# Another order of TensorE's and ScalarE's work in the last head of a cached-attention decode kernel

## The chip, the cores and the metric

The kernel runs on one core of a Trainium2 chip. The metric is the device time of one launch in microseconds (us). A core has five engines that run side by side, each through its own instructions in order: TensorE (PE: matmuls, with PEld for its weight loads), VectorE (DVE), ScalarE (ACT), GpSimd (POOL) and SyncE (SP, which here issues the loads from device memory). They meet only at semaphores.

## The reference, cut to what matters

One token is decoded. A block of attention over a cache of 32768 positions is followed by a small dense block:

```python
H, Sk, Dh, D, Dff = 32, 32768, 192, 640, 1536
q = (layernorm(x) @ wq).reshape(1, 1, H, Dh).transpose(0, 2, 1, 3)
p = softmax(einsum("bhqd,bhkd->bhqk", q, k_cache) * Dh ** -0.5)
o = einsum("bhqk,bhkd->bhqd", p, v_cache)
h = x + o.transpose(0, 2, 1, 3).reshape(1, 1, H * Dh) @ wo
out = h + relu(layernorm(h) @ w1) @ w2
```

All inputs are bf16. The two caches hold 32 heads x 32768 rows x 192 elements each, 805 MB together, and every element is used once. The page counts 824.97 MB read.

## The kernel before, in words

**One head.** The 32768 keys of a head lie on 128 partitions with 256 keys each. The work is cut into chunks: a chunk c is `jc` keys of every partition. Its scores are made in two ways. For the first `jc - jp` keys VectorE multiplies the keys by the query (L695) and sums each product (L698), into the tile `sc`. For the other `jp` keys TensorE transposes the keys (L373, into one of four PSUM tiles `tp`, four 128x128 blocks to a tile), ScalarE copies the transposed blocks to SBUF (L598, `kT`, two buffers by the chunk's parity), and TensorE multiplies them by the query (L354, into the one tile `sp`). ScalarE takes the exponentials of both parts (L604 from `sp` into `pB`, L613 from `sc` into `pA`) and sums them into `dsums` as it goes. TensorE then adds the value rows weighted by the exponentials (L354, `o_ps<-va,pB` and `o_ps<-va,pA`). The exponentials need no maximum, so a head has no second pass. The sum of the exponentials comes from a matmul with a matrix of ones (`den_mm`), its reciprocal from VectorE (L703, L704), which also scales the result (L710, `o_pair`); TensorE turns the pair of rows into a column (`o_turn`), VectorE copies that (L716, L720, `oT`), and TensorE multiplies it by `wo` (`project`) into the running sum `attT`.

**Order.** Heads 0 to 30 are a loop with a fixed order of eight chunks. The last head (`LAST`, 31) is written out in `pe_end` for TensorE, in the last part of `act_head` for ScalarE and in `dve_head` for VectorE. In what follows the steps of its ten chunks have short names, which the changed code uses too: T3 is `transposes` of chunk 3, C3 the copies of those blocks, S3 the `scores_pe` of chunk 3, E3 the exponential of TensorE's scores (`exp_pe`), D3 the exponential of VectorE's scores (`exp_dve`), P3 the value sums of chunk 3 (`values`), O the turn of the head before. P8 comes in two parts, P8a (the part of TensorE's scores) and P8b (the part of VectorE's); `den_mm` of the last head stands between them. Per chunk, `jp` is 16, 16, 20, 16, 20, 16, 12, 12, 8, 8 and VectorE's part is 16, 16, 12, 16, 12, 16, 8, 8, 8, 0 keys of a partition. So T and C have 12, 12, 15, 12, 15, 12, 9, 9, 6, 6 blocks, S has 24, 24, 30, 24, 30, 24, 18, 18, 12, 12 matmuls, and P has 16 matmuls in chunks 0 to 5, 10 in chunks 6 and 7, 8 in chunk 8 and 4 in chunk 9.

**What waits for what.** T waits for the keys and for the copy of the tile that used its PSUM bank four tiles earlier. C waits for its T. S waits for its last copy and for E of the chunk before, as there is one `sp`. E waits for S. D waits for VectorE. P waits for E and D of its chunk and for its values; P0 also waits until the head before has been scaled out of `o_ps` (L710). VectorE does its scores chunk after chunk; after chunk 0 it does L703, L704 and L710 of the head before, after chunk 2 it does L716 and L720, for which it needs O. VectorE waits for P0 before chunk 8 too.

**Loads.** All are issued by SyncE in one order (L235). For the last head: keys of chunks 0 and 1, values of chunks 0 and 1, keys of 2 and 3, keys of 4 and 5, values of 2 and 3, keys of 6 and 7, of 8, of 9, values of 4, of 5. Then come the values of chunks 6, 7, 8 and 9, which go over those of chunks 0 and 1 and so wait for P1 (L297); then the last piece of `wo`; then `w1` and four cuts of `w2` (6, 3, 2 and 1 of its 12 row blocks), which go over the keys of chunks 0 to 3 and wait for P3 (L303). GpSimd passes on the landing of the loads up to the values of chunk 3; for later ones TensorE and VectorE wait themselves.

**The end.** After P8b: L710, O, L720, `project`, the residual sum (L769), a layernorm (statistics by TensorE, square root by ScalarE at L626), `h1` (60 matmuls with `w1`), its relu (L668), `y` (60 matmuls with `w2`, waiting for each cut of it), the sum (L785), a transpose (L587), a copy (L671), the store (L673).

TensorE's order before, in these names: T0 T1 S0 P0 S1 T2 O P1 S2 T3 T4 S3 T5 S4 S5 P2 P3 T6 T7 S6 T8 S7 T9 S8 P4 S9 P5 P6 P7 P9 P8a den P8b. ScalarE's: C0 E0 D0 C1 E1 D1 C2 C3 E2 D2 C4 E3 C5 E4 D3 C6 E5 D4 C7 E6 C8 E7 D5 C9 E8 E9 D6 D7 D8.

Of the kernel before, what the change touches and what calls it, by code (L numbers as in the profile page):

```python
# [80 lines left out]
def kernel(  # L81
# [13 lines left out]
    P = nc.NUM_PARTITIONS  # L95

    Bsz, Sq, D = A_x.shape
# [18 lines left out]
    LAST = H - 1  # L116
# [12 lines left out]
    NCM = len(ends)  # L129
# [226 lines left out]
    def transposes(g, h, c):  # L356
        ld, off, jc, jp = chunks(h)[c][:4]
        src = k_tile(h, ld)
        if h == LAST and ld >= NL - 1:
            if c == 6 or ld >= NL:  # L360
                g.wait("k", h, ld)
        elif leads(h, c, 0):
            g.wait("at", "k", h, ld)
        t0 = sum(len(tiles(q[3])) for q in chunks(h)[:c])
        for k, (b0, nb) in enumerate(tiles(jp)):
            t = t0 + k
            dst = tp[t % TP]
            if t >= TP or h > 0:
                g.wait("cp", *tile_before(h, t))
            calls = []  # L370
            for b in range(nb):
                o = (off + jc - jp) * Dh + (b0 + b) * 2 * P
                calls.append(lambda b=b, o=o: pe.transpose(out=dst[:, b, :], in_=src[:, o:o + 2 * P].bitcast(f32),  # L373
                                                           identity=ident_f[:]))
            pe_group(g, calls, ("T", h, c, k), "pe_act")
# [11 lines left out]
    def scores_pe(g, h, c):  # L387
        ld, off, jc, jp = chunks(h)[c][:4]
        g.wait("cp", h, c, len(tiles(jp)) - 1)
        if c == 0:  # L390
            g.wait("qm", h)
        if c > 0:
            g.wait("ep", h, c - 1)
        elif h > 0:
            g.wait("ep", h - 1, NC - 1)
        src = kT[c % 2]
        calls = []
        for i in range(jp // 4):
            for b in range(3):
                for e in range(2):  # L400
                    calls.append(mmul(sp[:, 4 * i + b:4 * i + b + 2], src[:, 3 * i + b, e:2 * P:2],
                                      qm[:, 4 * b + 2 * e:4 * b + 2 * e + 2],
                                      start=(i == 0 and b == 0 and e == 0),
                                      stop=(i == jp // 4 - 1 and b == 2 and e == 1), skip_group_check=True))
        pe_group(g, calls, ("S", h, c), "pe_act")

    def values(g, h, c, part=None):


        jc, jp, ld, off = chunks(h)[c][2:]  # L410
        jd = jc - jp
        if h == LAST and ld >= NL - 1:
            g.wait("vc", h, c)
        elif h == LAST and ld == 2:
            g.wait("vh", c - 4)
        elif leads(h, c, 4):
            g.wait("at", "v", h, ld)
        g.wait("ep", h, c)
        if jd > 0 and part != 0:
            g.wait("ed", h, c)  # L420
        if c == 0 and h > 0:
            g.wait("os", h - 1)
        src = v_tile(h, ld)
        a, b = pA[c % NB], pB[c % NB]
        calls = []
        order = (list(range(jd, jc, 2)) if part != 1 else []) + (list(range(0, jd, 2)) if part != 0 else [])
        for i, j in enumerate(order):
            w = a[:, j:j + 2] if j < jd else b[:, j - jd:j - jd + 2]
            calls.append(mmul(o_ps[0:2, 0:2 * Dh], w, src[:, (off + j) * Dh:(off + j + 2) * Dh],
                              start=(c == 0 and i == 0),  # L430
                              stop=((c == NC - 1 if h < LAST else (c, part) == (NC, 1)) and i == len(order) - 1),
                              skip_group_check=True))
        pe_group(g, calls, ("PV", h, c) if part != 0 else ("PV0", h, c), "pe")
# [11 lines left out]
    def o_turn(g, h):  # L445
        g.wait("os", h)

        rows = [o_pair[:, i, :, :].rearrange("q a d -> q (a d)") for i in range(2)]
        pe_group(g, [mmul(mm[:, b:b + 1], rows[i][:, b:2 * Dh:3], ident_b[0:2, i:i + 1],
                          start=(i == 0), stop=(i == 1)) for b in range(3) for i in range(2)], ("oT", h), "pe_dve")  # L450
# [68 lines left out]
    def pe_start(g):  # L519
# [10 lines left out]
        g.wait("qe")  # L530
        q_spread(g, 0)

    def pe_end(g):
        h = LAST
        den_mm(g, h - 1)
        transposes(g, h, 0)
        transposes(g, h, 1)
        scores_pe(g, h, 0)
        values(g, h, 0)
        scores_pe(g, h, 1)  # L540
        transposes(g, h, 2)
        o_turn(g, h - 1)
        values(g, h, 1)
        scores_pe(g, h, 2)
        transposes(g, h, 3)
        transposes(g, h, 4)
        scores_pe(g, h, 3)
        transposes(g, h, 5)
        scores_pe(g, h, 4)
        scores_pe(g, h, 5)  # L550
        values(g, h, 2)
        values(g, h, 3)
        transposes(g, h, 6)
        transposes(g, h, 7)
        scores_pe(g, h, 6)
        transposes(g, h, 8)
        scores_pe(g, h, 7)
        transposes(g, h, 9)
        scores_pe(g, h, 8)
        values(g, h, 4)  # L560
        scores_pe(g, h, 9)
        for c in (5, 6, 7):
            values(g, h, c)
        values(g, h, 9)
        values(g, h, 8, 0)
        den_mm(g, h)
        values(g, h, 8, 1)
        o_turn(g, h)
        project(g, h + 1)
        st = ln_t["ln2"]["st"]  # L570
        g.wait("h_col")
        pe_group(g, [mmul(mm[:, 0:1], mean_mat[:], st[:, 0:1], start=True, stop=True)], ("mean", "ln2"), "pe_dve")
        g.wait("st", "ln2")
        pe_group(g, [mmul(sp[:, 0:2], mean_mat[:], st[:], start=True, stop=True)], ("mean2",), "pe_dve")
        g.wait("xn", "ln2")
        g.wait("w1")
        hn = ln_t["ln2"]["xn"]
        pe_group(g, [mmul(o_ps[:, f:f + 1], w1_s[:, c, f * P:(f + 1) * P], hn[:, c:c + 1],
                          start=(c == 0), stop=(c == DT - 1)) for f in range(FT) for c in range(DT)], ("h1",), "pe_act")
        g.wait("h1T")  # L580
        for i, (f0, f1) in enumerate(zip(W2_CUTS[:-1], W2_CUTS[1:])):
            g.wait("w2", i)
            pe_group(g, [mmul(attT[:, n:n + 1], w2_s[:, f, n * P:(n + 1) * P], h1T[:, f:f + 1],
                              start=(f == 0 and n == 0), stop=(f == FT - 1 and n == DT - 1), skip_group_check=True)
                         for f in range(f0, f1) for n in range(DT)], ("y", i), "pe_dve")
        g.wait("y_col")
        pe_group(g, [lambda: pe.transpose(out=mm[0:DT, 0:P], in_=y_col[:], identity=ident_f[:])], ("yT",), "pe_act")  # L587
# [4 lines left out]
    def copies(g, h, c):  # L592
        ld, off, jc, jp = chunks(h)[c][:4]
        t0 = sum(len(tiles(q[3])) for q in chunks(h)[:c])
        for k, (b0, nb) in enumerate(tiles(jp)):
            g.wait("T", h, c, k)
            src = tp[(t0 + k) % TP]
            g.do(lambda: act.copy(out=kT[c % 2][:, b0:b0 + nb, :], in_=src[:, 0:nb, :].bitcast(bf16)),  # L598
                 "act_pe", ("cp", h, c, k))

    def exp_pe(g, h, c):
        jp = chunks(h)[c][3]
        g.wait("S", h, c)
        g.do(lambda: act.activation(out=pB[c % NB][:, 0:jp], in_=sp[:, 0:jp], func=F.Exp, scale=SCALE,  # L604
                                    accum_out=dsums[:, 2 * c + 1:2 * c + 2]), "act_pe", ("ep", h, c))
# [29 lines left out]
    def act_head(g, h):  # L635
        q_wide(g, h)
        if h < LAST:
            for c in range(NC):
                if c == 4:
                    exp_pe(g, h, 3)  # L640
                    exp_dve(g, h, 3)
                copies(g, h, c)
                if c > 0 and c != 4:
                    exp_pe(g, h, c - 1)
                    exp_dve(g, h, c - 1)
            exp_pe(g, h, NC - 1)
            exp_dve(g, h, NC - 1)
            return

        behind = ((0,), (1,), (), (2,), (), (3,), (4,), (), (5,), ())  # L650
        for c in range(NCM):
            copies(g, h, c)
            if c < 2:
                exp_pe(g, h, c)
            elif c > 2:
                exp_pe(g, h, c - 1)
            for d in behind[c]:
                exp_dve(g, h, d)
        exp_pe(g, h, NCM - 1)
        for c in range(6, NCM):  # L660
            exp_dve(g, h, c)

    def act_end(g):
        act_head(g, LAST)
# [143 lines left out]
    for e in parts:  # L808
        far = {s: 0 for s in TAKEN[e]}
        ends_at[e] = []  # L810
        for h in range(LAST):
            for label in logs[e][h]:
                s, n = at[label]
# [90 lines left out]
```

The softmax here doesn't subtract the row's maximum and nothing guards it: scores larger than these inputs give would overflow.

## Time and profile before

| what | value |
|---|---|
| time, median of 6 runs | 1920.65 us (1919.46 to 1921.07) |
| time of the profiled execution | 1919.77 us |
| its span, first to last instruction | 1917.9 us |
| read from memory | 824.97 MB, 430 GB/s over the span |
| busy, share of the span | PE 83%, DVE 81%, ACT 49% |
| queue of the loads, share of 16 DMA engines | 99.6% |
| mean granted clock of TensorE | 0.898 |

The page gives shares over the whole span; the change touches only its last 65 us, so the views that matter are those cut to a stretch of time: the timeline of one engine (start, length, engine, line, operation, count; in brackets the idle time before it and what ended it), the chain of waits in order of time, the busy time and granted clock by stretches, and the issues of loads with the time from issue to landing. All times there are us from the start of the span.

### The profile page before, as it was taken

The numbers are of one execution on the slowest core, as the hardware profiler recorded it, in microseconds if no ns is written. First come the engines' busy times: TensorE is split into PE (matmuls) and PEld (weight loads), VectorE is DVE, ScalarE is ACT, GpSimd is POOL, SyncE is SP. The second block draws the span as 40 slices with busy tenths as digits, with TensorE's granted clock in tenths as the row PEclk, the third lists the DMA queues.
The fourth block names the chain that finished last, engine by engine and source line by source line (L and its number), as shares of the span: only waits on it lengthen the run. The fifth ranks groups of instructions, "written<-read, shape, count | busy, mean of one in ns | idle before, by whom it ended". The sixth has DMA issues, their size and how long they took to land.

```text
span 1917.9 us, 35954 instructions
## 1 busy us (share of the span) xinstructions
PE 1587.7 (83%) x15899; PEld 1003.2 (52%) x15899; DVE 1561.4 (81%) x731; ACT 936.6 (49%) x2000; POOL 1.0 (0%) x6
## 2 busy tenths in 40 slices
PE   7878888888888888788887887888888888878888
PEld 7555455555554555555554545545555555455455
DVE  2787887987878878789788888888798787887886
ACT  2454454553544544545545445445455354454454
POOL 0000000000000000000000000000000000000000
PEclk9889899898898898988888988989989889899898
DMA  9999999999999999999999999999999999999998
GB/s 408 435 438 427 436 431 433 437 429 439 431 435 437 431 437 431 434 437 432 436 432 433 438 431 436 433 433 437 431 437 429 436 435 433 436 434 433 435 428 330
DMA packets 25185, 825.28 MB, mean 430 GB/s; under 512 B 2635, under 2 KB 4172, under 8 KB 7628
## 3 DMA queue, kind: packets, MB, share of 16 engines
q1 hardware_dynamic: 25152, 824.98, 99.6%
q8 instruction: 15, 0.25, 0.0%
q14 instruction: 6, 0.05, 0.0%
q10 hardware_dynamic: 12, 0.00, 0.0%
HBM read 824.97 MB, written 0.00 MB: 430 GB/s over the span
## 4 chain that ended last, share of the span: by engine, by line
DMA 57%; DVE 37%; PE 3%; issue 1%; ACT 1%; DVEq 0%; SPq 0%; POOLq 0%
DMA kt<-in_A_k_cache_dram 51%; DVE pr L695 18%; DVE sc L698 18%; DMA va<-in_A_v_cache_dram 6%; PE o_ps L354 3%; ACT kT L598 1%; PE sp L354 0%; DVEq L65 0%; SPq L235 0%; PE attT L354 0%; PE mm L354 0%; DVE o_pair L710 0%; PE tp L373 0%; ACT pB L604 0%; POOLq L317 0%
## 5 line engine op out<-in xcount | busy, mean ns | idle before, releaser
L695 DVE TENSOR_TENSOR pr<-kt,qb 128x2304 f32<-128x2304 bf16 (+2 forms) x257 | 756.7, 2944 | 315.3 <-POOLq L317 293.9
L598 ACT COPY kT<-tp 128x1024 bf16<-128x1024 bf16 (+1 forms) x898 | 814.4, 1020 | 291.7 <-PE tp L373 291.7
L698 DVE TENSOR_REDUCE sc<-pr 128x12 f32<-128x2304 f32 (+2 forms) x257 | 756.1, 2942 | 8.9
L354 PE MATMUL o_ps<-va,pB 128*2 128x384 bf16 x2304 | 504.5, 373 | 178.8 <-POOLq L336 147.2
L373 PE MATMUL tp<-ident_f,kt 128*128 128x128 f32 x3456 | 520.7, 289 | 121.9 <-ACT kT L598 75.9
L373 PEld LDWEIGHTS tp<-ident_f,kt 128*128 128x128 f32 x3456 | 380.9, 144 | 222.4 <-ACT kT L598 169.2
L354 PEld LDWEIGHTS o_ps<-va,pB 128*2 128x2 bf16 x2304 | 199.5, 92 | 404.4 <-POOLq L336 152.6
L354 PE MATMUL o_ps<-va,pA 128*2 128x384 bf16 x1792 | 373.1, 353 | 0.0
L613 ACT ACTIVATE pA<-sc 128x12 bf16<-128x12 f32 (+2 forms) x257 | 58.9, 229 | 525.7 <-DVEq L65 525.7
L354 PEld LDWEIGHTS o_ps<-va,pA 128*2 128x2 bf16 x1792 | 162.9, 91 | 174.8 <-issue 57.1
L354 PEld LDWEIGHTS sp<-qm,kT 128*128 128x128 bf16 x6912 | 197.5, 97 | 79.3 <-ACT pB L604 30.2
L354 PE MATMUL sp<-qm,kT 128*128 128x2 bf16 x6912 | 213.2, 164 | 18.4 <-ACT pB L604 14.5
L604 ACT ACTIVATE pB<-sp 128x20 bf16<-128x20 f32 (+2 forms) x258 | 62.1, 241 | 115.0 <-PE sp L354 115.0
L604 ACT ACTIVATION_READ_ACCUMULATOR pB<-sp 128x1 f32 x258 | 64.5, 250 | 0.0
L613 ACT ACTIVATION_READ_ACCUMULATOR pA<-sc 128x1 f32 x257 | 52.8, 205 | 0.0
L354 PE MATMUL o_ps<-xn_ln,kt 128*96 128x1 bf16 (+1 forms) x316 | 22.3, 208 | 2.9 <-DMA kt<-in_A_wq_dram 2.8
L354 PEld LDWEIGHTS o_ps<-xn_ln,kt 128*96 128x96 bf16 (+1 forms) x316 | 22.2, 175 | 3.0 <-issue 2.9
L710 DVE TENSOR_SCALAR o_pair<-o_ps,rec 2x384 bf16<-2x384 f32 x32 | 19.4, 605 | 1.4 <-PE o_ps L354 0.4
L354 PEld LDWEIGHTS attT<-oT,wo_s 128*128 128x128 bf16 x465 | 13.6, 96 | 10.3 <-issue 9.9
L354 PE MATMUL attT<-oT,wo_s 128*128 128x1 bf16 x465 | 16.3, 164 | 0.3 <-DVE oT L720 0.3
L354 PEld LDWEIGHTS mm<-dsums,ones_mat 128*128 128x128 f32 x64 | 9.5, 188 | 10.6 <-issue 10.6
L703 DVE TENSOR_REDUCE rec<-mm 128x1 f32<-128x20 f32 x32 | 5.7, 179 | 10.4 <-PE mm L354 5.9
(65 smaller groups left out, 134.5 us busy)
## 6 DMA issues: line engine op xcount, KB each, us to landing
kt<-in_A_k_cache_dram SPq DMA_DIRECT2D x62, 6144.0 KB, 33.4
va<-in_A_v_cache_dram SPq DMA_DIRECT2D x62, 6144.0 KB, 20.9
kt<-in_A_k_cache_dram SPq DMA_DIRECT2D x3, 3072.0 KB, 24.6
wo_s<-in_A_wo_dram SPq DMA_DIRECT2D x16, 480.0 KB, 15.0
kt<-in_A_wq_dram SPq DMA_DIRECT2D x4, 1536.0 KB, 11.1
va<-in_A_v_cache_dram SPq DMA_DIRECT2D x2, 3072.0 KB, 27.6
va<-in_A_v_cache_dram SPq DMA_DIRECT2D x2, 1536.0 KB, 36.1
kt<-in_A_k_cache_dram SPq DMA_DIRECT2D x1, 1920.0 KB, 30.4
```

Source lines behind the costliest of these rows:

```text
L354: return lambda: pe.matmul(o, lhsT=w, rhs=r, **kw)
L373: calls.append(lambda b=b, o=o: pe.transpose(out=dst[:, b, :], in_=src[:, o:o + 2 * P].bitcast(f32), identity=ident_f[:]))
L598: g.do(lambda: act.copy(out=kT[c % 2][:, b0:b0 + nb, :], in_=src[:, 0:nb, :].bitcast(bf16)), "act_pe", ("cp", h, c, k))
L604: g.do(lambda: act.activation(out=pB[c % NB][:, 0:jp], in_=sp[:, 0:jp], func=F.Exp, scale=SCALE, accum_out=dsums[:, 2 * c + 1:2 * c + 2]), ...
L613: g.do(lambda: act.activation(out=pA[c % NB][:, 0:jd], in_=sc[c % NC][:, 0:jd], func=F.Exp, scale=SCALE, accum_out=dsums[:, 2 * c:2 * c + ...
L695: g.chain(lambda: dve.tensor_tensor(out=pr[:, 0:j1 - j0, :], in0=src[:, (off + j0) * Dh:(off + j1) * Dh].rearrange("p (j d) -> p j d", d=D ...
L698: g.chain(lambda: dve.reduce_sum(out=sc[c % NC][:, j0:j1], in_=pr[:, 0:j1 - j0, :], axis=X), "dve")
L703: g.chain(lambda: dve.reduce_sum(out=rec[:, 0:1], in_=mm[:, 0:2 * NCM], axis=X), "dve")
L710: g.do(lambda: dve.tensor_scalar_mul(out=o_pair[:, :, 1, :], in0=o_ps[0:2, 0:2 * Dh].rearrange("q (i d) -> q i d", i=2), scalar1=rec[0:2, ...
```

## The change

The hand-written order of the last head is replaced, on TensorE and on ScalarE, by two strings that a small helper walks through. No instruction is added or taken away, and no operand, load or wait of an instruction is edited; VectorE's, GpSimd's and SyncE's programs are untouched. The waits themselves follow their steps.

```diff
+    LAST_PE = "T0 T1 S0 T2 S1 T3 S2 P0 O S3 T4 T5 S4 P1 S5 P2 T6 P3 S6 T7 T8 P4 S7 T9 S8 P5 S9 P6 P7 P9"
+    LAST_ACT = "C0 C1 E0 D0 C2 E1 C3 E2 D1 E3 D2 C4 C5 E4 D3 E5 C6 E6 D4 C7 C8 E7 D5 C9 E8 D6 E9 D7 D8"
+
+    def run(g, steps, table):
+        for s in steps.split():
+            table[s[0]](g, LAST, *([int(s[1:])] if s[1:] else []))
+
     def pe_end(g):
         h = LAST
         den_mm(g, h - 1)
-        transposes(g, h, 0)
-        transposes(g, h, 1)
-        scores_pe(g, h, 0)
-        values(g, h, 0)
-        scores_pe(g, h, 1)
-        transposes(g, h, 2)
...
-        for c in (5, 6, 7):
-            values(g, h, c)
-        values(g, h, 9)
+        run(g, LAST_PE, {"T": transposes, "S": scores_pe, "P": values, "O": lambda g, h: o_turn(g, h - 1)})
         values(g, h, 8, 0)
         den_mm(g, h)
         values(g, h, 8, 1)
@@
-        behind = ((0,), (1,), (), (2,), (), (3,), (4,), (), (5,), ())
-        for c in range(NCM):
-            copies(g, h, c)
...
-        exp_pe(g, h, NCM - 1)
-        for c in range(6, NCM):
-            exp_dve(g, h, c)
+        run(g, LAST_ACT, {"C": copies, "E": exp_pe, "D": exp_dve})
```

On TensorE, P0 moves behind T2, S1, T3 and S2; P1 behind S3, T4, T5 and S4; P2 ahead of T6, with S5 between it and P1; P3 behind T6; P4 ahead of S7, T9 and S8; P5 ahead of S9. On ScalarE, C1 moves ahead of E0, C3 ahead of D1, D2 and E3 ahead of C4, C5 ahead of E4, D3 and E5 ahead of C6, and C8 ahead of E7.

More of the change, by code (lines that the diff above doesn't have):

```diff
@@ L535, in pe_end @@
         den_mm(g, h - 1)
-        transposes(g, h, 0)
-        transposes(g, h, 1)
-        scores_pe(g, h, 0)
-        values(g, h, 0)
-        scores_pe(g, h, 1)
-        transposes(g, h, 2)
[L542 to L561, printed above, removed]
-        for c in (5, 6, 7):
-            values(g, h, c)
-        values(g, h, 9)
+        run(g, LAST_PE, {"T": transposes, "S": scores_pe, "P": values, "O": lambda g, h: o_turn(g, h - 1)})
         values(g, h, 8, 0)
@@ L648, in act_head @@
             return
-        behind = ((0,), (1,), (), (2,), (), (3,), (4,), (), (5,), ())
-        for c in range(NCM):
-            copies(g, h, c)
[L653 to L658, printed above, removed]
-        exp_pe(g, h, NCM - 1)
-        for c in range(6, NCM):
-            exp_dve(g, h, c)
+        run(g, LAST_ACT, {"C": copies, "E": exp_pe, "D": exp_dve})
     def act_end(g):
```

## The prediction

> **What bounds the kernel now.** The page says loads at 99.6% of the DMA engines, so the heads before the last are bound by memory and the change cannot touch them. I read the last head alone. First the chain of waits from 1850 us on (start, length, what):
>
> ```profile
> 1881.08 6.84 PE o_ps L354 x32
> ...
> 1895.47 3.88 PE o_ps L354 x16
> 1899.35 0.39 PE sp L354 x12
> 1899.73 7.24 PE o_ps L354 x44
> 1906.97 0.33 PE mm L354 x2
> 1907.30 0.75 PE o_ps L354 x4
> ```
>
> From 1895.4 on the end is a row of value sums on TensorE: P4, then P5 P6 P7 P9 P8a without a gap, then den and P8b. Second, VectorE's timeline:
>
> ```profile
> 1899.67 1.75 DVE L698 TENSOR_REDUCE sc<-pr 128x8 f32<-128x1536 f32 x1
> 1907.34 0.18 DVE L703 TENSOR_REDUCE rec<-mm 128x1 f32<-128x20 f32 x1 [5.92 <-PE mm L354]
> ```
>
> Its last scores are done at 1901.42, and it stands for 5.92 us until TensorE has worked off its backlog. From 1850.66 to 1901.42 it waits at most 0.22 us at once: that is the floor for the last head. Third, where TensorE lost the time, and what ScalarE did then:
>
> ```profile
> 1880.31 0.77 PE L354 MATMUL sp<-qm,kT 128*128 128x2 bf16 x24 [2.00 <-ACT pB L604]
> 1881.01 3.34 PE L354 MATMUL o_ps<-va,pB 128*2 128x384 bf16 x10
> ```
> ```profile
> 1888.55 2.20 ACT L598 COPY kT<-tp 128x1024 bf16<-128x1024 bf16 x3 [8.09 <-PE tp L373]
> ```
>
> P2 and P3 stand in one block ahead of T6, so ScalarE has nothing to copy for 8.09 us, and S6 to S9 come late and with them E8 and E9. Ahead of P2, TensorE waits. Fourth, the clock (length, PE, PEld, DVE, ACT, POOL busy with counts, then TensorE's clock, DMA share, GB/s):
>
> ```profile
> 1873.95:1877.36 3.41, 2.57 (x37) 1.77 (x33) 3.38 (x2) 3.41 (x7) 0.00 (x0) 1.00 0.97 414
> 1877.36:1880.78 3.42, 1.37 (x49) 1.29 (x50) 3.27 (x2) 3.09 (x7) 0.00 (x0) 1.00 0.97 402
> 1880.78:1884.19 3.41, 3.41 (x23) 1.45 (x20) 3.23 (x3) 0.00 (x0) 0.00 (x0) 0.50 1.06 441
> ...
> 1894.43:1897.84 3.41, 3.34 (x23) 1.46 (x22) 3.19 (x2) 2.25 (x9) 0.00 (x0) 0.50 1.01 409
> ```
>
> A stretch in which TensorE has little to do is followed by one at half clock, and value sums pay for it: ten took 3.34 us at 1881.01, while ten at full clock take 1.62 (P6, 1902.26 to 1903.88). Last, the loads:
>
> ```profile
> 1907.00:1910.00 3.00, 1.88 (x27) 1.12 (x27) 1.30 (x6) 0.00 (x0) 0.00 (x0) 1.00 0.35 125
> ```
> ```profile
> kt<-in_B_w_dram SPq DMA_DIRECT2D x1, 160.0 KB, 7.6
> ```
>
> The DMA engines run full until 1907 and fade out by 1910. The last cut of w2, issued at 1902.0, lands 7.6 us later, at 1909.6. This is a second floor, close above the first.
>
> **The change, step by step.** Nothing is added, so I lay the same steps out in the new order with lengths from the rows. On TensorE: T of 12 blocks 1.5 us and of 15 1.77 (1862.02 to 1863.79); S of 24, 30, 18 and 12 matmuls 0.62, 0.76, 0.47 and 0.38; P of 16, 10 and 4 matmuls 2.69 (1858.71 to 1861.40), 1.62 and 0.65. On ScalarE: copies of 12, 15, 9 and 6 blocks 2.73, 3.43, 2.1 and 1.4; E 0.17, D 0.19. A released engine starts 0.05 to 0.1 late. Landings are issue plus time to landing: keys of chunk 2 1825.99+35.8=1861.8, of chunk 4 1850.06+19.5=1869.6, of chunk 6 1850.90+30.4=1881.3; values of chunk 2 1850.43+26.3=1876.7, of 4 1853.25+34.4=1887.7, of 5 1853.62+37.8=1891.4, of 6 to 9 by 1869.78+29.0=1898.8.
>
> *Front part.* To S0 (1856.97 to 1857.7) all is as now. Then T2 stands ahead of P0, and its keys land at 1861.8: TensorE idles 4.2 us, with S1, T3, S2 and P0 queued behind, where today P0 runs at 1858.71. T2 from 1861.9, S1 at 1863.7; C2 from 1862.5 to 1866.0, S2 at 1866.3, P0 1867.1 to 1869.8, O done at 1870.1. VectorE asks for O at 1870.93, so the loss is covered with 0.8 us to spare. If that cover goes, VectorE's floor moves one for one.
>
> *Middle.* S3; T4 from 1870.5. On ScalarE, C4 is now behind D2, whose scores end at 1870.51, so it starts at 1870.9, C5 ends by 1877.3. S4 at 1874.7, P1 1875.4 to 1878.0, S5, P2 1878.7 to 1881.3, T6 from 1881.4 (its keys), P3 1882.4 to 1885.0. So P2 and P3 end 2.8 us earlier than now (1887.85), with T6 done as well, and ScalarE's gap ahead of C6 shrinks from 8.1 to about 3 us.
>
> *End.* S6 T7 T8 to 1887.6; P4 1887.8 (its values have just landed) to 1890.4; S7 T9 S8 to 1891.9; P5 to 1894.5; S9 to 1894.9; P6 to 1896.5. P7 needs VectorE's chunk 7, done at 1897.65: D7, then P7 1898.1 to 1899.7, P9 to 1900.4, P8a to 1901.0. From here TensorE waits for VectorE, not the other way round. Chunk 8 is done at 1901.42, D8 at 1901.8, den at 1901.9, P8b 1902.2 to 1903.0. Today P8b ends at 1907.23+0.81=1908.04: 5.0 us.
>
> *Loads.* Two steps move past SyncE's waits. P1 ends at 1878.0 instead of 1868.4, so values 6 to 9 are issued 9.6 us later. Ahead of them in the queue lie loads that keep it busy until 1891.4, 13 us more, and now SyncE stalls while it issues them (the last takes it 5.1 us, until 1874.9), so I cost this at nothing. P3 ends 2.8 us earlier, and w1 can be issued sooner; with full DMA engines this moves no landing, so I cost it at nothing too. The bounds are a landing 0.5 us earlier (the fading stretch of 1907 to 1910 filled a little) and 9.6 us later (the delay passed on whole); I take zero, by the full DMA share at the time.
>
> *Behind P8b.* Every step keeps its distance, so h1 would start at 1910.80-5.0=1905.8 (w1 lands 1887.95+16.7=1904.65, in time) and y at 1912.87-5.0=1907.9. The cuts of w2 land at 1907.1, 1908.4, 1909.2 and 1909.6. The last cut's five matmuls, 0.14 us, with 0.1 for the release and 0.165 for the last to end, bring y to 1910.0. It ends at 1912.87+1.76=1914.63 now. **The sum is 4.6 us**: 5.0 from TensorE's backlog, of which the transfers take back 0.4. Against the profiled execution, 1919.77-4.6=1915.2 us (a span of 1913.3). That execution lies 0.9 under the median of the six; carried along, this is 1916.0.
>
> **The clock, and a rule against the change.** The price I can't read off is the clock behind the new idle gap. Behind an idle stretch of 2.63 us in the head before, at 1811.03, ten value sums took 3.36 us. So T2 may run at half clock, which hardly costs it. But P0 at half clock takes up to 5.4 us, O comes at 1872.8, 1.9 us too late, and the sum falls to 5.0-1.9=3.1. Against that, T2 and T3 bring 27 transposes ahead of P0, and after 1873.95 to 1877.36, with 12 transposes, 18 scores and no value sum, the clock stayed 1.00. I take the full clock, by that row, and keep 3.1 as the other end.
>
> The Trainium skill ("TensorE: Matmul & The Clock Gate", section "HAM oscillation — how this bites in real kernels") asks for no idle gap over about 3.4 us, and its Part 4, "PE-mode transpose", says that transposes don't count as busy for the clock in the same way. By both, P0 would run at half clock and the gain would be 3.1 us; the row from 1873.95 contradicts the second, since transposes alone held the clock there.
>
> **The rivals.**
>
> *Half clock for P0.* O late, VectorE late by up to 1.9 us, a gain of about 3.1: 1917.5. For it speaks the gap of 4.2 us; against it the 27 transposes.
>
> *Given back at the end.* The steps move but their waits don't go: E and D queue behind copies, P4, P5 or P7 start late, or w2 lands later. TensorE's stop before P7 leaves 1.5 us and that before P8b 0.9, so a slip up to 2.4 us is swallowed before 1897 and more counts whole. A gain of 0 to 2.5, say 1919.4. Against it: ScalarE has some 28 us of work in these 50 (108 blocks at 0.228, 19 exponentials at 0.17 to 0.19), and the floor at 1901.42 isn't moved.
>
> *Slower: the loads run dry.* The four value loads wait for P1. If the queue has drained before they get through, every later landing moves, w2 last. All 9.6 us of delay would put w2 at 1919.2, y at 1919.6, 5.0 later than now: 1925.6. It decides from 4.6 us of idle DMA on, that is if the queue needed some 18 us from issue to the first byte. Against it stand the 13 us queued.
>
> **How the numbers follow.** Forecast 0.65 (1914.9 to 1916.8), half clock 0.18, given back 0.10, run dry 0.07. About 0.2%, 3.8 us, can be told from no change here, so half clock, given back and 0.02 of run dry count as the same: faster 0.65, same 0.30, slower 0.05. The range takes in the forecast, half clock and half of given back: 1914.9 to 1919.2.
>
> **What would show it.** Right: T2 near 1862 behind a gap of some 4 us; L720 near 1870.9; VectorE's last L698 ending near 1901.4 with L703 within 1 us; value loads issued near 1878 with the DMA share unbroken; y waiting for w2. Wrong: L720 after 1871.5, an idle DMA stretch after 1885, or L703 still 2 us or more behind L698.

## The result, and the profile after

The changed kernel takes 1915.66 us (median of 16 runs, 1915.13 to 1915.90) against 1920.38 for the kernel before (36 runs, 1918.24 to 1921.68): a ratio of 0.9975, with a 95% interval of 0.9969 to 0.9982. That is 4.7 us. The profiled execution took 1915.21 us, with a span of 1913.2. The runs also lie closer together: 0.8 us from lowest to highest instead of 3.4.

The chain of waits of the changed kernel, where the chain of before was one row of value sums from 1895.4 on:

```profile
1897.81 1.77 DVE pr L663
1899.60 1.76 DVE sc L666
1901.44 0.31 ACT pA L592 x2
1901.80 0.40 PE mm L354 x2
1902.19 0.75 PE o_ps L354 x4
...
1907.45 0.28 ACT h1T L636
1907.78 1.36 PE attT L354 x45
1909.14 0.31 issue
1909.45 0.56 PE attT L354 x15
1910.03 0.17 DVE y_col L753
```

From 1850.59 to 1901.36 it is VectorE's scores (L663 and L666 are L695 and L698 of before); then D8, den and P8b follow at once. P8b starts at 1902.12 and is the last of the value sums: 1902.12+0.81=1902.93, against 1908.04. Inside y there is a stop of 0.31 us ahead of the last 15 matmuls, those that need the last two cuts of w2. The profile names nothing that ended this stop; the last cut, issued near 1901.8 and landing 7.6 us later, near 1909.4, fits it. VectorE's timeline says the same at the two places that the prediction named:

```profile
1870.86 0.22 DVE L688 TENSOR_SCALAR oT<-mm,odd 128x3 bf16<-128x3 f32 x1
...
1902.23 0.18 DVE L671 TENSOR_REDUCE rec<-mm 128x1 f32<-128x20 f32 x1 [0.88 <-PE mm L354]
```

The copy of O (L688, before L720) has no bracket, so VectorE did not wait for it, and the wait ahead of the reciprocal is 0.88 us where it was 5.92. ScalarE's long stop is shorter too:

```profile
1883.18 2.20 ACT L577 COPY kT<-tp 128x1024 bf16<-128x1024 bf16 x3 [3.00 <-PE tp L373]
```

TensorE's timeline of the front part shows the gap that the prediction placed there, and what it costs:

```profile
1857.74 0.75 PE L354 MATMUL sp<-qm,kT 128*128 128x2 bf16 x24 [0.26 <-ACT kT L577]
1861.77 3.36 PE L373 MATMUL tp<-ident_f,kt 128*128 128x128 f32 x15 [3.28 <-POOLq L336]
...
1867.76 1.46 PE L354 MATMUL o_ps<-va,pB 128*2 128x384 bf16 x8
1869.06 1.46 PE L354 MATMUL o_ps<-va,pA 128*2 128x384 bf16 x8
1870.46 0.31 PE L354 MATMUL mm<-wide,o_pair 2*128 2x1 bf16 x6
```

T2 starts at 1861.77 behind 3.28 us of waiting for the keys. It takes 3.15 us to the start of S1 (1864.92) where it took 1.77 before. P0 runs at full speed, and O ends at 1870.77, 0.09 us ahead of VectorE. S3 stands behind O, and ScalarE's timeline shows E3 waiting for it, and the copies C4 and C5 starting behind E3 and D2:

```profile
1871.49 0.18 ACT L583 ACTIVATE pB<-sp 128x16 bf16<-128x16 f32 x1 [1.85 <-PE sp L354]
...
1871.99 6.30 ACT L577 COPY kT<-tp 128x1024 bf16<-128x1024 bf16 x7
```

Last the clock, in stretches (length, PE, PEld, DVE, ACT, POOL busy with counts, TensorE's clock, DMA share, GB/s):

```profile
1860.30:1863.70 3.40, 1.93 (x10) 1.93 (x11) 3.37 (x2) 1.38 (x6) 0.00 (x0) 0.74 1.04 448
1863.70:1867.10 3.40, 3.40 (x50) 3.33 (x49) 3.25 (x2) 3.40 (x7) 0.00 (x0) 0.76 0.97 419
1867.10:1870.50 3.40, 3.40 (x48) 1.95 (x44) 3.31 (x2) 2.54 (x7) 0.00 (x0) 1.00 1.02 431
...
1881.00:1903.00 22.00, 21.08 (x182) 12.03 (x180) 19.92 (x12) 10.71 (x29) 0.00 (x0) 1.00 1.02 421
```

The same view of before, from P2 to the end of the value sums:

```profile
1881.00:1908.00 27.00, 25.51 (x191) 13.62 (x188) 19.96 (x11) 10.37 (x31) 0.00 (x0) 0.88 1.00 409
```

After the change the half clock falls on T2 and S1, far from the end, and the last 22 us run at 1.00. Before, it fell twice on value sums that the end waited for. How long TensorE was busy does not alone tell when the half clock comes. Before, the stretch ahead of P4's half clock had 2.49 us of work, hardly less than the 2.57 us of the one from 1873.95, which was followed by full clock:

```profile
1891.02:1894.43 3.41, 2.49 (x47) 2.03 (x48) 3.23 (x3) 3.41 (x8) 0.00 (x0) 1.00 1.01 423
```

What sets it is not shown here.

### The profile page after: what moved, and what is told of

The parts are those of the page before. It is cut to its first block, busy times and chain, and to the rows that moved or that the text cites. A ratio compares the mean times of both kernels' runs of the same rounds, so it can differ in the third digit from the quotient of the medians.

```text
span 1913.2 us, 35954 instructions
## 1 busy us (share of the span) xinstructions
PE 1581.4 (83%) x15899; PEld 992.3 (52%) x15899; DVE 1561.4 (82%) x731; ACT 938.1 (49%) x2000; POOL 1.0 (0%) x6
## 4 chain that ended last, share of the span: by engine, by line
DMA 55%; DVE 41%; PE 2%; issue 1%; DVEq 0%; POOLq 0%; ACT 0%; SPq 0%
DMA kt<-in_A_k_cache_dram 55%; DVE pr L663 20%; DVE sc L666 20%; PE o_ps L354 1%; DMA kt<-in_A_wq_dram 0%; DVEq L65 0%; PE attT L354 0%; DVE o_pair L678 0%; PE mm L354 0%; POOLq L317 0%; POOLq L336 0%; DVE oT L688 0%; PE mm L566 0%; ACT pA L592 0%; ACT h1T L636 0%
## 5 line engine op out<-in xcount | busy, mean ns | idle before, releaser
L663 DVE TENSOR_TENSOR pr<-kt,qb 128x2304 f32<-128x2304 bf16 (+2 forms) x257 | 756.7, 2944 | 315.3 <-POOLq L317 293.9
L666 DVE TENSOR_REDUCE sc<-pr 128x12 f32<-128x2304 f32 (+2 forms) x257 | 756.1, 2942 | 8.9
L373 PE MATMUL tp<-ident_f,kt 128*128 128x128 f32 x3456 | 511.2, 284 | 119.1 <-ACT kT L577 79.5
L373 PEld LDWEIGHTS tp<-ident_f,kt 128*128 128x128 f32 x3456 | 370.7, 142 | 222.3 <-ACT kT L577 174.4
```

Source lines behind the costliest of these rows:

```text
L663: g.chain(lambda: dve.tensor_tensor(out=pr[:, 0:j1 - j0, :], in0=src[:, (off + j0) * Dh:(off + j1) * Dh].rearrange("p (j d) -> p j d", d=D ...
L666: g.chain(lambda: dve.reduce_sum(out=sc[c % NC][:, j0:j1], in_=pr[:, 0:j1 - j0, :], axis=X), "dve")
```

## The experiments

My theory was that VectorE's chain is the floor, the last landing of w2 a second one just above it, and that the change takes TensorE's backlog of value sums out of the end. The rival explanations were that the gain is the clock and not the order; that one part of the change carries it alone; and, for the risks, that a late issue of loads or a late O does no harm, or harm in full. Each kernel was timed beside the kernel before, whose medians in the three sets were 1920.57, 1920.25 and 1920.58. The changed kernel was not timed again in them, so differences from its 1915.66 are between sets, and the kernel before lay up to 0.2 us from its own 1920.38 there.

**TensorE's new order alone.** The string of ScalarE is put back to its old order.

```diff
-    LAST_ACT = "C0 C1 E0 D0 C2 E1 C3 E2 D1 E3 D2 C4 C5 E4 D3 E5 C6 E6 D4 C7 C8 E7 D5 C9 E8 D6 E9 D7 D8"
+    LAST_ACT = "C0 E0 D0 C1 E1 D1 C2 C3 E2 D2 C4 E3 C5 E4 D3 C6 E5 D4 C7 E6 C8 E7 D5 C9 E8 E9 D6 D7 D8"
```

> TensorE's new order with ScalarE's old one. My theory: VectorE's chain is the floor, and the new TensorE order needs the copies ahead. With the old ScalarE order, C2 stands behind D1, whose scores VectorE ends near 1865.2, so S2 and P0 come late, O ends near 1873 to 1875, and L720 and all of VectorE after it move 2 to 4 us later: L720 near 1873 to 1875, about 1917.5 to 1920. Rival (TensorE's order alone carries the gain): L720 stays near 1870.9 and the time near 1915.7.

Measured: 1919.01 us (1917.97 to 1921.83), ratio 0.9994 (0.9985 to 1.0003), no change that can be told. VectorE's timeline:

```profile
1875.78 0.22 DVE L688 TENSOR_SCALAR oT<-mm,odd 128x3 bf16<-128x3 f32 x1 [4.95 <-PE mm L354]
1908.80 0.18 DVE L671 TENSOR_REDUCE rec<-mm 128x1 f32<-128x20 f32 x1 [2.52 <-PE mm L354]
```

This is one of the four longest of the eleven runs (1921.2 to 1921.8; the other seven took 1918.0 to 1919.6), so its waits need not be those of the others. C2 behind D1 puts S2 2.9 us later than in the changed kernel, at 1869.81. P0, from 1870.72 on, then runs at half clock and takes 4.71 us instead of 2.69. VectorE stands 4.95 us for O. TensorE's order needs ScalarE's copies ahead.

**The new front, the old back.** From P2 on, TensorE has its old order, and ScalarE from C6 on.

```diff
-... S5 P2 T6 P3 S6 T7 T8 P4 S7 T9 S8 P5 S9 P6 P7 P9"
+... S5 P2 P3 T6 T7 S6 T8 S7 T9 S8 P4 S9 P5 P6 P7 P9"
-... E5 C6 E6 D4 C7 C8 E7 D5 C9 E8 D6 E9 D7 D8"
+... C6 E5 D4 C7 E6 C8 E7 D5 C9 E8 E9 D6 D7 D8"
```

> The changed kernel with the old order from P2 on (P2 P3 in one block ahead of T6, P4 behind S8, and ScalarE's old order from C6 on). My theory: the new front gives TensorE 2 us more ahead of P2, so P2 and P3 run at full clock and end near 1884; the slack ahead of P7 takes up most of the rest, and P8b ends near 1903 to 1904: 1915.7 to 1916.7. Rival (the gain is that P2/P3 and P4/P5 are no longer in blocks): close to the kernel before, 1919 to 1920.

Measured: 1917.55 us (1917.13 to 1919.23), ratio 0.9989 (0.9980 to 0.9998). Between the two expectations, about a microsecond over mine. TensorE's timeline shows P2 at full speed, but P4 not:

```profile
1880.19 1.79 PE L354 MATMUL o_ps<-va,pB 128*2 128x384 bf16 x10
...
1891.06 0.60 PE L354 MATMUL sp<-qm,kT 128*128 128x2 bf16 x18 [0.92 <-ACT pB L583]
...
1893.03 3.24 PE L354 MATMUL o_ps<-va,pB 128*2 128x384 bf16 x10
```
```profile
1905.24 0.18 DVE L671 TENSOR_REDUCE rec<-mm 128x1 f32<-128x20 f32 x1 [3.47 <-PE mm L354]
```

Behind the stretch of transposes and scores ahead of P4, with its stop of 0.92 us, P4 still meets the half clock, and VectorE still waits 3.47 us for the backlog.

**The old front, the new back.** The kernel before up to S4, then the new order, with P2 ahead of S5.

```diff
-    LAST_PE = "T0 T1 S0 T2 S1 T3 S2 P0 O S3 T4 T5 S4 P1 S5 P2 T6 P3 ..."
+    LAST_PE = "T0 T1 S0 P0 S1 T2 O P1 S2 T3 T4 S3 T5 S4 P2 S5 T6 P3 ..."
-    LAST_ACT = "C0 C1 E0 D0 C2 E1 C3 E2 D1 E3 D2 C4 C5 E4 D3 E5 ..."
+    LAST_ACT = "C0 E0 D0 C1 E1 D1 C2 C3 E2 D2 C4 E3 C5 E4 D3 E5 ..."
```

> The kernel before up to S4, and the new order from there (P2 S5 T6 P3 S6 T7 T8 P4 S7 T9 S8 P5 S9, with ScalarE's new order from E5 on). My theory: P2 starts near 1878.2 and fills the idle time ahead of S5, P4 and P5 run while ScalarE copies, P8b ends near 1903 to 1904 behind VectorE: 1915.7 to 1916.7. Rival (the copies ahead in the first chunks carry the gain): 1918.5 to 1920.

Measured: 1915.57 us (1915.26 to 1916.15), ratio 0.9975 (0.9965 to 0.9985): the whole gain. The copies ahead in the first chunks, which most of the diff is about, are not what the time needs, once P2 to P5 stand between the later steps. TensorE's timeline:

```profile
1878.55 3.35 PE L354 MATMUL o_ps<-va,pB 128*2 128x384 bf16 x10
...
1889.91 1.79 PE L354 MATMUL o_ps<-va,pB 128*2 128x384 bf16 x10
...
1902.17 0.40 PE L354 MATMUL mm<-dsums,ones_mat 128*128 128x20 f32 x2 [0.24 <-ACT pA L592]
```

P2 meets the half clock in this execution as it did before (3.35 us for its ten first sums), and still den waits for D8, so TensorE has no backlog left. P2 starts at 1878.55 instead of 1881.01, in what was the stop ahead of S5, and P4 runs at full clock. The new order has room for one half clock.

**The clock alone.** The kernel before, with matmuls that nobody reads in two of TensorE's stops.

```diff
+    def filler(g, n):
+        for _ in range(n):
+            g.do(mmul(attT[0:2, 256:512], ident_b[:, 0:2], wide[:, 0:256], start=False, stop=False, skip_group_check=True))
         scores_pe(g, h, 4)
+        filler(g, 16)
         scores_pe(g, h, 5)
...
         transposes(g, h, 8)
+        filler(g, 7)
         scores_pe(g, h, 7)
```

> The kernel before, with 16 idle matmuls of 256 columns ahead of S5 and 7 ahead of S7, where TensorE stands still for 2.0 and 0.9 us; they write PSUM columns that nothing reads. Order untouched, only the clock can change. If the order alone is the cause: no half clock or not, the backlog stays and the time is 1920 to 1921, at best 0.5 less. If the half clock over P2 and over P4 is the cause (3.34 and 2.98 us for ten sums instead of 1.62): 3.1 us less, 1917.3, with the ten first sums of P2 and of P4 in 1.8 us each.

Measured: 1917.13 us (1916.71 to 1918.18), ratio 0.9982 (0.9973 to 0.9991), 3.4 us less than before with more work in the program. TensorE's timeline and VectorE's wait:

```profile
1878.24 3.34 PE L354 MATMUL attT<-wide 128*2 128x256 bf16 x16
...
1882.23 1.79 PE L354 MATMUL o_ps<-va,pB 128*2 128x384 bf16 x10
...
1895.05 1.79 PE L354 MATMUL o_ps<-va,pB 128*2 128x384 bf16 x10
```
```profile
1905.80 0.18 DVE L709 TENSOR_REDUCE rec<-mm 128x1 f32<-128x20 f32 x1 [4.38 <-PE mm L354]
```

The half clock now falls once, on the first filler, and the first sums of P2 and P4 take 1.79 us each instead of 3.34 and 2.98. In this execution the filler itself ran at half clock and overran its stop, so that S5 started at 1881.51 instead of 1880.31; a wait of 4.38 us is left, and its span of 1916.4 is the longest of its eleven runs. By the medians, 3.4 us come back with the old order once the half clock is off the value sums, and the change is another 1.5 us faster (1917.13 against 1915.66). The two rows of sums account for 1.55+1.19=2.7 us of the 3.4; this execution, the longest, does not show the rest.

**P0 back ahead of T2.**

```diff
-    LAST_PE = "T0 T1 S0 T2 S1 T3 S2 P0 O S3 ..."
+    LAST_PE = "T0 T1 S0 P0 T2 S1 T3 S2 O S3 ..."
```

> The changed kernel with P0 back ahead of T2 (right behind S0). My theory: the front part of the change gives nothing to the time; P0 fills the gap in which TensorE waits for the keys of chunk 2, T2 to S2 run at full clock, O comes near 1867 instead of 1870.5, and VectorE's chain is the same: 1915.2 to 1916.2, with 3 us instead of 0.1 us between O and L720. Rival (holding P0 back is part of the gain, since TensorE gets to T2 or S1 sooner): 0.5 us or more slower than the changed kernel.

Measured: 1916.58 us (1915.54 to 1917.43), ratio 0.9980 (0.9971 to 0.9989). My expectation failed, the rival's 0.5 us or more came true, and not by its reason:

```profile
1860.83 1.82 PE L354 MATMUL o_ps<-va,pB 128*2 128x384 bf16 x8 [2.40 <-ACT pA L592]
1862.45 2.77 PE L354 MATMUL o_ps<-va,pA 128*2 128x384 bf16 x8
...
1873.19 5.90 PE L373 MATMUL tp<-ident_f,kt 128*128 128x128 f32 x27
```

P0 needs E0 and D0, and in the new ScalarE order these stand behind C1. P0 so waits until 1860.8, runs partly at half clock (4.3 us instead of 2.69), and pushes T2 from 1861.8 to 1865.2; the next stop brings another half clock, in which T4 and T5 take 5.9 us. O still ends in time (1870.76), so VectorE is not late; TensorE is, and L671 waits 3.22 us for it. Ten of the eleven runs are longer than the longest of the changed kernel. Holding P0 back belongs with C1 ahead of E0: one goes with the other.

**O late.** O moves behind S4.

```diff
-    LAST_PE = "T0 T1 S0 T2 S1 T3 S2 P0 O S3 T4 T5 S4 P1 ..."
+    LAST_PE = "T0 T1 S0 T2 S1 T3 S2 P0 S3 T4 T5 S4 O P1 ..."
```

> The changed kernel with O moved behind S4. My theory: VectorE's chain sets the end, one for one: S4 ends near 1876, O and L720 near 1876.3, 5.4 us later than now, L703 and all behind it 5.4 us later; 0.4 of it is swallowed by the wait for w2: 1920.2 to 1921. Rival (TensorE's value sums set the end, VectorE has slack): 1915.7 to 1917.

Measured: 1920.83 us (1920.20 to 1921.65), ratio 1.0004 (0.9995 to 1.0013); 5.2 us over the changed kernel.

```profile
1877.12 0.22 DVE L688 TENSOR_SCALAR oT<-mm,odd 128x3 bf16<-128x3 f32 x1 [6.19 <-PE mm L354]
...
1908.49 0.18 DVE L671 TENSOR_REDUCE rec<-mm 128x1 f32<-128x20 f32 x1 [0.88 <-PE mm L354]
```

L688 is 6.26 us later than in the changed kernel, L671 6.26 us later, one for one, with the same 0.88 us behind VectorE. The span is 6.1 us longer, as the stop inside y is gone; by the medians it is 5.2: the execution shown lies 0.3 us above its median, that of the changed kernel 0.45 below.

**The value loads later still.** They wait for P3, then for P4, instead of P1.

```diff
-                    g.wait("PV", LAST, 1)
+                    g.wait("PV", LAST, 3)      # the first; 4 in the second
```

> The changed kernel with the loads of the values of chunks 6 to 9 waiting for P3 instead of P1, so that they are issued near 1886.4, 7.2 us later still. My theory: what is queued ahead lasts to 1888 on the first engine and 1891 on the last, so the queue idles 1 us at most: 1915.5 to 1916.7. Rival (a late issue passes on whole): 1922.5.

> The same loads waiting for P4, so issued near 1891.6, when the queue has just run empty. My theory: the DMA engines idle from 1888 to 1891 on until the first new bytes, 2.5 to 4 us, w2 lands near 1912 to 1913, y waits for it, and the time is 1918 to 1919.7. Rival (a late issue passes on whole, 12.4 us): 1927. Other rival (TensorE's sums set the end and w2 has slack): 1915.7 to 1916.5.

Measured: 1915.73 us (1915.32 to 1916.02), ratio 0.9978 (0.9969 to 0.9987), and 1919.75 us (1918.64 to 1920.29), ratio 0.9996 (0.9987 to 1.0005). The first, issued from 1886.8 on, changes nothing. The second, issued from 1891.56 on, lets the DMA engines run dry (stretches as above, the DMA share in the last column but one). TensorE then waits for values ahead of P6, P7 and P8a (0.30, 0.53 and 1.02 us), for w1 (0.71 us) and for w2:

```profile
1888.00:1890.00 2.00, 1.88 (x13) 0.92 (x12) 2.00 (x1) 2.00 (x4) 0.00 (x0) 1.00 0.48 199
1890.00:1892.00 2.00, 2.00 (x29) 1.13 (x27) 1.85 (x2) 0.95 (x2) 0.00 (x0) 1.00 0.06 25
```
```profile
1911.03 0.94 PE L354 MATMUL attT<-h1T,kt 128*128 128x1 bf16 x30 [1.77 <-DMA kt<-in_B_w_dram]
```

A late issue costs nothing while the queue is full, and about the time that the engines stand still when it is not: 2x0.52+2x0.94=2.9 us in these two rows, for 3.7 us more of span and 4.1 us more of median. The changed kernel issues these loads at 1879.21, with its DMA share unbroken, so the rival of the loads that run dry was at least 7.6 us of further delay away, as 1886.8 is still free.

**The two floors.** Half of w2; half of w2 and less of chunk 8 on VectorE; all of w2 and less of chunk 8. The first two leave the second half of w2 out of the computation and use the first half twice.

```diff
-        for i, (c0, c1) in enumerate(zip(W2_CUTS[:-1], W2_CUTS[1:])):
+        for i, (c0, c1) in enumerate(zip(W2_CUTS[:2], W2_CUTS[1:2])):      # first and second
-                              w2_s[:, f, n * P:(n + 1) * P]
+                              w2_s[:, f % (FT // 2), n * P:(n + 1) * P]     # first and second
-    ends += [..., (NL, 0, 16, 8), (NL + 1, 0, 8, 8)]
+    ends += [..., (NL, 0, 16, 12), (NL + 1, 0, 8, 8)]                       # second and third
```

> The changed kernel that loads only the first half of w2 and uses it twice (the second half of w2 is left out of the computation, the matmuls stay). My theory: behind VectorE's floor there is a second one, the landing of w2, which takes back 0.4 us; without it y runs through: 1915.0 to 1915.4, no stop inside y. Rival (the sums of TensorE alone set the end): the same as the changed kernel, 1915.7.

> The same half of w2, and in chunk 8 VectorE does 4 keys of a partition instead of 8 (TensorE 12). My theory: both floors are lowered; VectorE ends near 1899.6 instead of 1901.4, TensorE's sums then follow by 1901.9 instead of 1902.9, and with w2 no longer late the time is 1913.9 to 1914.6. Rival (a third thing holds the end): as with half of w2 alone.

> All of w2, and chunk 8 with 4 keys of a partition for VectorE. My theory: P8b ends 1 us earlier, but y then waits 1 us longer for w2: no gain, 1915.3 to 1915.8. Rival (w2 has slack): 1914.5 to 1914.9.

Measured: 1915.11 us (1914.80 to 1915.71), 1915.34 (1914.39 to 1915.94) and 1915.19 (1914.58 to 1915.67), ratios 0.9974 (0.9963 to 0.9984), 0.9972 (0.9962 to 0.9982) and 0.9973 (0.9963 to 0.9984). Half of w2 lies in the expected range. Its 0.5 us under the changed kernel are between sets and the ranges overlap; the firmer sign is that y runs through, in 1.76 us, where it took 2.2 with its stop (1907.78 to 1909.99):

```profile
1908.06 1.76 PE L354 MATMUL attT<-h1T,kt 128*128 128x1 bf16 x60 [0.36 <-ACT h1T L636]
```

Less of chunk 8 gives nothing on top of half of w2, against my expectation of 1 us and as its rival had it. With all of w2 it is 0.1 us under my range, but not by my reason. I had P8b ending 1 us earlier and y waiting longer for w2; in its profile, the longest of its eight runs, P8b ends 1 us later (1903.96) and y runs through:

```profile
1871.85 0.22 DVE L688 TENSOR_SCALAR oT<-mm,odd 128x3 bf16<-128x3 f32 x1 [1.00 <-PE mm L354]
...
1903.59 0.18 DVE L671 TENSOR_REDUCE rec<-mm 128x1 f32<-128x20 f32 x1 [2.85 <-PE mm L354]
```

TensorE is the end again, 2.85 us behind VectorE. O was late by 1.00 us, T7 and T8 have 18 blocks instead of 15, and P6 to P8a stand in a row from 1898.18 on, P9 and P8a now with 10 matmuls together instead of 8. In the changed kernel VectorE's scores, TensorE's sums and the last landing are each within about a microsecond of setting the end. Of the full versions the last has the lowest median, 0.5 us under the changed kernel, with ranges that overlap: no clear gain.

**w2 in longer pieces.** A partition's rows of w2 lie side by side, and w1's columns are read with a step of 12.

```diff
-            load(w2_s[:, c0:c1], B_w2.rearrange("(c p) n -> p c n", p=P)[:, c0:c1], ...
+            load(w2_s[:, c0:c1], B_w2.rearrange("(p c) n -> p c n", p=P)[:, c0:c1], ...
-        ... w1_s[:, c, f * P:(f + 1) * P], hn ...
+        ... w1_s[:, c, f:Dff:FT], hn ...
```

> The changed kernel with the hidden units dealt out so that a partition's rows of w2 lie side by side in memory (w1's columns are then read with a step of 12). My theory: the cuts of w2 come in pieces of 1280 to 7680 bytes instead of 1280, the DMA engines move them at the 430 GB/s of the caches instead of 400, w2 lands 0.2 to 0.4 us earlier and the time is 1915.1 to 1915.5. Rival (weights read with a step load slower): h1 takes more than 1.72 us, 1916 or more.

Measured: 1917.09 us (1916.80 to 1917.65), ratio 0.9984 (0.9975 to 0.9993), 1.4 us more than the changed kernel. The rival was right:

```profile
1906.09 3.77 PE L354 MATMUL o_ps<-xn_ln,kt 128*128 128x1 bf16 x60
```

h1 takes 3.77 us instead of 1.72. The clock is not the reason: 13 of its matmuls run in 0.60 us at a clock of 1.00 (from 1906.7) and 13 at 0.50 (from 1907.9). This costs more than an earlier w2 can give. Whether the longer pieces alone gain is left open.

## Why the prediction was right, and where not

**The sum.** 5.0 us from TensorE's backlog less 0.4 for w2 gave 4.6; the profiled executions differ by 1919.77-1915.21=4.6, the medians by 4.7. P8b was put at 1902.2 to 1903.0 and ran from 1902.12 to 1902.93; y was to end at 1910.0, and L753 follows it at 1910.03. With half of w2 the stop inside y was gone, which speaks for the second floor; its size, 0.4 us in the sum, is too near the 0.2 us between sets to be told from the times. That the profiled execution met the sum to 0.1 us is partly luck, as the next parts show.

**What bounds the last head.** Right, and shown in two ways: O late moves the end one for one, and with the change the reciprocal follows VectorE within 0.9 us. VectorE no longer stands for the backlog, and P7 and den wait for its scores, as laid out.

**Why the gain arises.** Here the prediction was incomplete. It named the half clock over P2 and P4 in its reading, but its sum laid out steps at full clock and booked all 5.0 us as backlog. The filler kernel shows that 3.4 us come back with the old order when the half clock is moved off the value sums. That does not make 3.4 us of the gain clock and 1.5 us order: with the old front and the new back P2 still ran at half clock, and the whole gain was there, as P2 filled a stop and only P4 was spared. Each cure alone takes most of the same backlog away, and VectorE's floor caps what both give together, so the shares depend on which is taken first. The prediction's reading that a stretch with little to do brings the half clock fits P2 (1.37 us of work ahead of it) and not P4 (2.49). Nor is the 3.4 us of idle time that it quotes a bound here: the half clock came behind stops of 2.00 us (P2) and 0.92 us (P4).

The spread of the runs goes the same way (3.4 us for the kernel before, 1.5 with the filler, 0.8 for the change, 0.9 for the new back alone); that the clock makes it is likely, but no run shows it.

**The front part.** "T2 may run at half clock, which hardly costs it" is the step that failed. T2 took 3.15 us instead of 1.77, O ended at 1870.77 instead of 1870.1, and the 0.8 us to spare were 0.09. Besides the changed kernel, seven of the kernels profiled have the same front up to O; in five of them VectorE waits for O, 0.39 to 1.17 us. So the 0.09 us were luck, and VectorE's floor does move by such waits. P0 itself ran at full clock, as chosen, in all eight profiles. The row from 1873.95, by which it was chosen, has scores beside its transposes, so "transposes alone" said too much of it; the stretch at the end of this document has only transposes. The rival of half clock had its gap (3.28 us, where the sum had 4.2) and its half clock; what saved the time is that it fell on T2 rather than on P0. Its price is seen with TensorE's order alone, where P0 at half clock took 2.0 us more.

**The middle.** The layout was early from P1 to P6, by 1.0 to 1.3 us (P1 1876.42 instead of 1875.4, P6 1896.19 instead of 1894.9). It let C4 wait for D2 alone and start at 1870.9. E3 also stands ahead of it and waits for S3, which the late front moved to 1871.45, so C4 started at 1871.99, and S4 and P1 followed. The stop of 1.5 us ahead of P7 swallowed this: P7 was put at 1898.1 and started at 1898.12, with 0.15 us of stop left. The prediction had said that a slip of up to 2.4 us would be swallowed, and that is why the end came true although the middle was late.

**The parts.** The prediction did not say which part is needed. The new back alone gives the whole gain. The new front alone gives 2 to 3 us (by ratio and by medians), and its TensorE half needs ScalarE's. P0 has to be held back where C1 is ahead of E0; with both in their old places, as in the new back, nothing was lost.

**The loads.** Costed at nothing, and nothing they cost: issued at 1879.21 instead of 1868.46, without SyncE's stall, and w1 as soon as P3 ended. That 13 us of queue cover the delay was right; the price of running dry is about the time that the engines stand still (4.1 us of median for 12.4 us of delay), not the whole delay, so that rival was also priced too high.

## What to carry to other kernels

Before counting instructions behind a late engine, look at its clock there: behind a stop or a stretch of small work the next large matmuls can cost double (ten sums 3.15 us instead of 1.62 here). Spreading the large ones between the small ones, or even idle work in the stop, gave most of it back, and an order with room ahead of the floor can bear it. A static order on two engines is one thing: a step moved on the one is paid or wasted by what stands ahead of its input on the other, so try the halves, and ask for the part that is needed. When one chain is the floor, list what comes just above it (here a landing that already costs 0.3 us, and TensorE's sums, 0.6 us ahead of the D8 that den waits for), because that is where the gain will stop.

## What the runs showed of the hardware

Transposes run at about half speed under half clock: T2's 15 took 3.15 us instead of 1.77, and 27 took 5.9 us, 0.21 each instead of 0.12. They also count as work for the clock. In the kernel with P0 ahead of T2 a stretch of transposes alone at 0.50 was followed by one at 1.00:

```profile
1875.40:1878.80 3.40, 3.40 (x18) 3.40 (x17) 3.25 (x2) 3.40 (x5) 0.00 (x0) 0.50 0.96 411
1878.90:1882.20 3.30, 3.30 (x48) 2.08 (x46) 3.27 (x2) 2.09 (x6) 0.00 (x0) 1.00 1.00 413
```

The Trainium skill ("TensorE: Matmul & The Clock Gate", Part 4, "PE-mode transpose") says that the full clock does not engage for transposes; here, with transposes of f32 blocks where the times on that page are for bf16, it did, and the measurement decides.

Weights read with a step cost more than double: 60 weight loads with a step of 12 elements took 3.69 us, one every 62 ns, against 1.64 us, one every 27 ns, with the columns side by side.
